# Two-level second product: another order of VectorE's sums, two outer sums left on GpSimd, the first group's weight sums in buffers of their own

## The chip, the cores and the metric

The kernel runs on one core of one Trainium2 chip. The metric is device time in microseconds (us) of one execution. The engines are TensorE (PE; its weight loads are listed as PEld), VectorE (DVE), ScalarE (ACT), GpSimd (POOL) and SyncE (SP), which only issues DMAs here. All data is float32.

## What is computed

Linear attention without softmax, with an RMS norm per head, and behind it a token mixer and a channel mixer. Batch 8, 8 heads of 64, sequence 576:

```python
kv = np.einsum('bhsd,bhse->bhde', k, v)
out = np.einsum('bhsd,bhde->bhse', q, kv)
x = out / np.sqrt(np.mean(out * out, axis=-1, keepdims=True) + 1e-06) * g_norm
# x to (8, 576, 512): heads side by side
h = np.maximum(x.transpose(0, 2, 1) @ w_tok1, 0.0) @ w_tok2     # 576 -> 256 -> 576
u = x + h.transpose(0, 2, 1)
h2 = np.maximum(u @ w_ch1, 0.0) @ w_ch2                         # 512 -> 1536 -> 512
return u + h2
```

The change touches only the channel mixer, the last two matrix products and the sums around them.

## The kernel before

**Stages.** Attention and token mixing fill the first third of the run and leave u in nine groups of 512 rows in DRAM (one per batch element, and one of the remaining 64 rows of all). The channel mixer then takes the groups one after the other. For each it computes v = relu(u @ w_ch1) and then v @ w_ch2, which is added to u.

**Winograd's form of Strassen's product.** Both products are done with seven block products instead of eight. With factors cut in 2 by 2 blocks, four sums of one factor's blocks (S1 to S4) and four of the other's (T1 to T4) are made first, then products numbered 1 to 7, and seven more additions put the result together. Group 0 does this on one level (`channel1_once`, `channel2_once`). Groups 1 to 8 do it on two: each of the seven *outer* products is made of seven *inner* ones, 49 for each matrix product, 98 for a group. One inner product is three matmuls of 128x128x128, which the trace shows as six records.

**Who does which sums.** Sums within one outer product are *inner* sums, sums between the blocks of the whole matrix *outer* sums.

- The weights' sums are made once, during group 0, by `split` (lines 283 to 297). For every outer product it makes three inner sums in a tile, writes the tile to DRAM (`last`, line 293), and leaves a fourth sum to be made in place (`steps[2]`). Later `fetch_sums` (line 679) fetches one tile for each outer product of each group, three ahead, into the three buffers of the pool `sums`. In the kernel before `split` takes its tiles from these same three buffers (`sums_tile`, line 280).
- The sums of the activations u, transposed in the tile uT, are made by `outer_u` and `inner_u` (lines 457 to 463) on VectorE.
- The results of the first product, v, lie in tiles v1 to v7. `outer` (line 614) runs one outer product: the inner products 1, 6, 7 and 4 accumulate in one PSUM bank a, 5 and 3 in b, 2 in c. Behind each product on a the running sum is read out by `read` (line 633): into t1, u2, u3 and then to the result's lower left part. ScalarE copies, or, where a *base* is given (line 704), VectorE reads and adds the base. Three writes by VectorE (`write`, line 642) add b or c to t1, u2 and u3. The next product on a can't start before the read of the last one, and the second on b not before the write of the first. `tmp` has one buffer for t1, two for u2 and one for u3.
- The remaining outer sums of v are made by `padd` (line 712) on GpSimd: v3 += v1, v2 += v1, v1 = v4 + v3 and v7 = v5 + v4, each in two halves of 128x768.
- ScalarE applies the relu to v2, v7 and v1 (`rectify`, line 716). The other outer sums of the second product (`make_a21`, `sum1` to `sum4`) are VectorE's, with the relu of v6 in them.
- The inner sums of v for the second product are made by `inner(o)` (line 760) on VectorE: three in a tile sv (three buffers), and one in place, or in a tile sv3 for outer product 1 (`own`).
- The second product's results r are added to each other (`radd`) and to xg (`xadd`), the tile with u, which is then stored in two halves; `fetch_x` fetches the next group's xg into the same tile.

**Order.** The order of work is written out by hand in *places*. A group has 98 of them, one inner product each. Outer product i of the first matrix product (order 1, 6, 2, 7, 5, 3, 4) has its inner products at places 7i + 0, 1, 3, 4, 6, 9 and 12 for p = 1, 2, 6, 5, 7, 4 and 3 (`PLACE`, line 608); the next outer product fills the gaps. The second matrix product (order 1, 4, 6, 5, 7, 2, 3) follows from place 49 on. `put(place, step)` says behind which inner product a step is issued. In the code b is the group's place 0 in `channel1` and its place 49 in `channel2`, so b + 59 there is place 10 of the next group. Steps at one place are issued in the order of their `put`s. Every engine takes its own instructions strictly in the order in which they are issued, and `keep` holds them in it. The writes of an outer product stand at 7i + 2 (c), 7i + 8 (first use of b) and 7i + 13 (second use of b).

The transposes of the next group (`turn_u`) stand at places 60, 64, 68 and 72, the next group's first sums of uT at 89, 91, 95 and 102, and the fetches of weight sums for the outer product three ahead at 7n + 13.

**The start of the two-level part.** During group 0's second product, `weave` (line 857) issues the steps of group 1's preparation between the products: first the last sums for group 0's own weights, then the in-place sums of the seven weights w_ch1, then the sums of the seven weights w_ch2 with their writes to DRAM. After it come the fetches of xg and of the first three tiles of weight sums (lines 985 to 987), and then the places of group 1.

Of the kernel before, what the change touches and what calls it, by code (L numbers as in the profile page):

```python
# [18 lines left out]
def kernel(  # L19
# [32 lines left out]
    nc = tc.nc  # L52
# [67 lines left out]
    def relu(o, a):  # L120
        keep(nc.scalar.activation(o, a, AF.Relu))  # L121
# [158 lines left out]
    def sums_tile():  # L280
        return late["sums"].tile([P, 3, FQ], F32, name="sums", tag="sums")

    def split(weight, o):


        at = []
        steps = (s_sums if weight == 1 else t_sums)(lambda n: part(weight, o, n, at[0]))

        def first():
            at.append(sums_tile())  # L290
            steps[0]()

        def last():
            steps[3]()
            dma(sums_dram[weight, o], at[0])

        return [first, steps[1], last], steps[2]
# [313 lines left out]
    def put(place, *steps):  # L611
        beside[place] += steps
# [52 lines left out]
    def sub(t, i, j):  # L665

        return t[:, ts(i, W), j]
# [22 lines left out]
    def channel1(g, n0):  # L690


        b = 7 * n0

        def first(i, o):
            n = n0 + i

            def mul(p, ps, start, stop):
                for w in range(W):
                    matmul(ps[:, ts(w, P)], lhsT=part(1, o, p, sums[n])[:, ts(w, P)],  # L700
                           rhs=uT[g][:, SB[o], SB[p]], start=(start and w == 0), stop=stop,
                           skip_group_check=True)

            base = {5: 3, 4: 1}.get(o)
            outer(7 * n, FQ, mul, lambda i, j: sub(v_tile(g, TO[o]), i, j),
                  base and (lambda i, j: sub(v_tile(g, base), i, j)))
            put(7 * n + PLACE[3] + 1, do(fetch_sums, n + 3))

        for i, o in enumerate(ORDER1):
            first(i, o)  # L710

        def padd(o, x, y):
            return halves(lambda i: tensor_add(*(half(v_tile(g, t), i) for t in (o, x, y)),
                                               engine=nc.gpsimd))

        def rectify(t, *places):
            for i in range(2):
                for j in range(2):
                    put(b + places[i], lambda i=i, j=j: relu(*2 * [sub(v_tile(g, t), i, j)]))


        put(b + 22, *padd(3, 3, 1))
        put(b + 29, *padd(2, 2, 1))
        put(b + 36, *padd(1, 4, 3))
        put(b + 43, *padd(7, 5, 4))
        rectify(2, 36, 39)
        rectify(7, 47, 48)
        rectify(1, 57, 58)
        if g > 1:
            steps = outer_u(g) + inner_u(g, 2, 7)  # L730
            for place, step in zip((0, 0, 2, 3, 4, 5, 7, 9), steps):
                put(b + place, step)

    def channel2(g, n0):
        b = 7 * n0
        t = {n: do(v_tile, g, i) for n, i in FROM.items()}

        def second(i, o):
            n = n0 + i
            r = {}  # L740

            def mul(p, ps, start, stop):
                v = v_in_parts[g, o](p)
# [12 lines left out]
            return r  # L756

        rs = {o: second(i, o) for i, o in enumerate(ORDER2)}

        def inner(o):  # L760


            got = {}

            def v_part(p):
                if p in (5, 6, 3):
                    return got[0][:, {5: 0, 6: 1, 3: 2}[p]]
# [12 lines left out]
            def own():  # L780
                a21 = sub(t[o](), 0, 1)
                got[7] = late["s3"].tile([P, W, P], F32, name="sv3")
                tensor_add(got[7], v_part(1), a21, ALU.subtract)

            return [begin, steps[1], steps[3]], own if o == 1 else steps[2]

        ins = {o: inner(o) for o in ORDER2}
        n1, n2, n3, n4, n5, n6, n7 = (t[n] for n in range(1, 8))
        a21 = n7

        def sum1(i):
            keep(nc.vector.scalar_tensor_tensor(out=half(n5(), i), in0=half(a21(), i), scalar=0.0,
                                                in1=half(n4(), i), op0=ALU.max, op1=ALU.add))

        def sum2(i):
            tensor_add(half(n6(), i), half(n5(), i), half(n1(), i), ALU.subtract)

        def sum3(i):

            keep(nc.vector.scalar_tensor_tensor(out=half(n7(), i), in0=half(a21(), i), scalar=0.0,  # L800
                                                in1=half(n1(), i), op0=ALU.max, op1=ALU.subtract))

        def sum4(i):
            tensor_add(half(n3(), i), half(n2(), i), half(n6(), i), ALU.subtract)

        def make_a21(i):
            tensor_add(half(a21(), i), half(a21(), i), half(v_tile(g, 5), i))

        put(b - 8, *ins[1][0], ins[1][1])
        put(b + 1, *halves(make_a21))  # L810
        put(b + 4, *ins[4][0])
        put(b + 6, *halves(sum1))
        put(b + 9, ins[4][1], *halves(sum2))
        put(b + 12, *ins[6][0])
        put(b + 15, *halves(sum4))
        put(b + 17, ins[6][1], *ins[5][0])
        put(b + 20, ins[5][1], *halves(sum3))
        put(b + 24, *ins[7][0], ins[7][1])
        put(b + 28, *ins[2][0], ins[2][1])
        put(b + 33, *ins[3][0], ins[3][1])  # L820


        quarter = lambda i, j: xg[g][:, 2 * i:2 * i + 2, ts(j, DH)]
        radd = lambda o, a: do(lambda: tensor_add(rs[o][0], rs[o][0], rs[a][0]))
        xadd = lambda i, j, o: do(lambda: tensor_add(quarter(i, j), quarter(i, j), rs[o][0]))
        put(b + 22, xadd(0, 0, 1))
        put(b + 23, xadd(1, 0, 4))
        put(b + 29, radd(6, 1))
        put(b + 31, xadd(0, 1, 6))
        put(b + 36, xadd(0, 1, 5))  # L830
        put(b + 38, xadd(1, 1, 5))
        put(b + 43, radd(7, 6))
        put(b + 52, xadd(1, 0, 7), xadd(1, 1, 7))
        put(b + 59, xadd(0, 0, 2), do(store, g, xg, 1))
        put(b + 63, xadd(0, 1, 3), do(store, g, xg, 0), do(fetch_x, g + 1))


        for i in range(J):
            place = b + 12 + 4 * i
            put(place - 12, do(fetch_t, g + 1, i)) if i < 2 else None  # L840
            put(place - 1, do(turn_u, g + 1, i, t_psum))
            put(place, do(fetch_t, g + 1, i + 2)) if i < 2 else None
        for i, step in enumerate(inner_u(g + 1, 0, 2)):

            put(b + (53 if i == 2 else 40 + 2 * i), step)

    def store(g, x, i):
        x = x[g]
# [129 lines left out]
    inner1 = [split(1, o) for o in ORDER1]  # L978
    inner2 = [split(2, o) for o in ORDER2]
    weave(channel1_once(0), firsts + [f for fs, _ in inner1 for f in fs])  # L980
    extra = [do(turn, 1, i, t_psum) for i in range(J)]
    extra += [lambda: [f() for f in outer_u(1)], lambda: [f() for f in inner_u(1, 0, 7)], lambda: None]
    body = [step for pair in zip(channel2_once(0), extra) for step in pair]
    weave(body, lasts + [f for _, f in inner1] + [f for fs, _ in inner2 for f in fs])
    fetch_x(1)
    for n in range(3):
        fetch_sums(n)


    for n, (_, f) in enumerate(inner2):  # L990
# [44 lines left out]
```

## Time and profile before

| | us |
|---|---|
| median of 3 runs | 978.64 |
| the runs | 974.67, 978.64, 981.25 |
| the profiled execution | 981.5 |
| its span, first to last instruction | 979.6 |
| mean granted TensorE clock | 0.945 |

| busy in the span | us | share |
|---|---|---|
| TensorE matmul | 861.8 | 88% |
| VectorE | 724.5 | 74% |
| ScalarE | 331.1 | 34% |
| GpSimd | 122.1 | 12% |

The two-level part goes from 336.6 us to 972 us. The profile's tables name a group of instructions by line, engine, operation and tiles; L118, L121, L124 and L127 are the helpers through which all additions, relus, copies and matmuls go, so the tiles tell them apart: `t<-ps_a,v` is a read of bank a into t1 with a base, `v<-ps_b,u` a write from b, `sv<-sv,v` an inner sum for the second product, `uT<-uT` a sum of the activations. A wait reads: who, for whom, how long in all, how often, the longest one. In the order of time a line gives start, duration, engine, line, operation, shape and count, and in brackets the idle time before it with what ended it.

### The profile page before, as it was taken

To read this page: it belongs to the slowest core of one execution; us is meant where nothing else is said; L and a number is where in the kernel's file an instruction comes from. 1 tells how busy PE (TensorE), PEld (TensorE's weight loads), DVE (VectorE), ACT (ScalarE), POOL (GpSimd) and SP (SyncE) were. 2 spreads that over 40 slices of the span, in tenths; PEclk is the share of its full clock that TensorE was granted. 3 is DMA by queue.
4 is the path that set the end of the run, shared out by engine and by line. 5 is a ranking of instruction groups with operands and counts; after the bars stand their busy time and mean duration, and the time that the engine had idled before them with its cause. 6 is when DMAs were issued, how large, how long until landed. Compare 5 with 4: busy or idle time off the path is not lost.

```text
span 979.6 us, 16051 instructions
## 1 busy us (share of the span) xinstructions
PE 861.8 (88%) x6144; PEld 761.1 (78%) x6144; DVE 724.5 (74%) x1384; ACT 331.1 (34%) x924; POOL 122.1 (12%) x78
## 2 busy tenths in 40 slices
PE   6478997979999868998998999899899799899896
PEld 6255564644588768998998999899899799899896
DVE  2568887988786835985885885886796697598585
ACT  2556545455111022323324223323323233332321
POOL 1000000000000005006006004102302300500600
PEclk9789898989999978999999899899899899999998
DMA  9975776422422453444535444335345344454432
GB/s 306 322 249 183 258 229 221 162 86 96 156 107 90 161 200 99 162 139 157 165 119 186 141 143 162 135 127 184 117 143 187 115 144 143 144 171 140 153 122 68
DMA packets 66924, 156.53 MB, mean 160 GB/s; under 512 B 5280, under 2 KB 23712, under 8 KB 66848
## 3 DMA queue, kind: packets, MB, share of 16 engines
q1 hardware_dynamic: 65488, 154.29, 46.8%
q10 hardware_dynamic: 1360, 1.21, 0.4%
q8 instruction: 49, 0.80, 0.3%
q14 instruction: 27, 0.22, 0.1%
HBM read 128.35 MB, written 27.13 MB: 159 GB/s over the span
## 4 chain that ended last, share of the span: by engine, by line
PE 53%; DVE 28%; DMA 9%; issue 4%; ACT 4%; SPq 0%; DVEq 0%; ACTq 0%
PE ps_a L127 19%; PE ps_b L127 10%; DVE v L118 7%; DVE sv L118 7%; PE ps_u L127 5%; PE ps_h L127 5%; PE ps_c L127 4%; DMA sums<-sums 4%; PE ps_v L127 4%; PE ps_w L127 3%; ACT x L351 2%; DVE xg L118 2%; DVE uT L118 2%; DVE r L118 2%; DMA out_dram<-xg 2%
## 5 line engine op out<-in xcount | busy, mean ns | idle before, releaser
L118 POOL TENSOR_TENSOR v<-v,v 128x768 f32<-128x768 f32 x64 | 119.4, 1892 | 803.9 <-DVE v L118 779.0
L124 ACT COPY u<-ps_a 128x384 f32<-128x384 f32 (+1 forms) x192 | 67.9, 354 | 213.0 <-PE ps_a L127 194.7
L118 DVE TENSOR_TENSOR v<-ps_b,u 128x384 f32<-128x384 f32 x112 | 60.5, 552 | 60.8 <-PE ps_b L127 44.1
L127 PE MATMUL ps_a<-uT,sums 128*128 128x128 f32 x336 | 54.5, 304 | 48.1 <-DVE t L118 30.0
L127 PE MATMUL ps_b<-uT,sums 128*128 128x128 f32 x672 | 95.5, 296 | 0.0
L127 PEld LDWEIGHTS ps_b<-uT,sums 128*128 128x128 f32 x672 | 90.3, 212 | 0.0
L127 PE MATMUL ps_a<-uT,w_ch 128*128 128x128 f32 x576 | 83.5, 286 | 7.0 <-DVE uT L118 7.0
L127 PEld LDWEIGHTS ps_a<-uT,sums 128*128 128x128 f32 x336 | 47.4, 213 | 51.0 <-DVE t L118 31.5
L127 PEld LDWEIGHTS ps_a<-uT,w_ch 128*128 128x128 f32 x576 | 76.0, 202 | 8.2 <-issue 8.1
L351 ACT ACTIVATE x<-x,inv 128x64 f32<-128x64 f32 x288 | 70.9, 335 | 17.0 <-DVE inv L347 16.9
L124 ACT COPY t<-ps_a 128x384 f32<-128x384 f32 (+1 forms) x96 | 34.0, 354 | 124.0 <-PE ps_a L127 123.7
L127 PE MATMUL ps_h<-x,w_tok 128*128 128x512 f32 (+1 forms) x160 | 67.3, 613 | 5.1 <-DVE w_tok L118 5.1
L127 PE MATMUL ps_u<-h,w_tok 128*128 128x512 f32 (+1 forms) x160 | 71.7, 640 | 0.0
L118 DVE TENSOR_TENSOR uT<-uT 128x512 f32<-128x512 f32 (+3 forms) x96 | 62.6, 663 | 2.7 <-ACT uT L124 1.9
L121 ACT ACTIVATE v<-v 128x384 f32<-128x384 f32 (+1 forms) x102 | 49.5, 527 | 28.4 <-DVE v L118 20.0
L127 PE MATMUL ps_a<-uT,w 128*128 128x128 f32 x432 | 59.0, 276 | 0.0
L118 DVE TENSOR_TENSOR u<-ps_a,v 128x384 f32<-128x384 f32 x32 | 17.8, 558 | 52.5 <-PE ps_a L127 52.5
L127 PEld LDWEIGHTS ps_h<-x,w_tok 128*128 128x128 f32 (+1 forms) x160 | 26.8, 195 | 35.8 <-issue 34.2
L127 PEld LDWEIGHTS ps_a<-uT,w 128*128 128x128 f32 x432 | 53.8, 193 | 0.0
L127 PEld LDWEIGHTS ps_u<-h,w_tok 128*128 128x128 f32 (+1 forms) x160 | 27.4, 195 | 33.8 <-issue 31.6
L127 PEld LDWEIGHTS ps_kv<-v_in,k_in 128*128 128x128 f32 x320 | 40.1, 203 | 14.8 <-DMA v_in<-in_v_dram 6.3
L127 PEld LDWEIGHTS ps_o<-kvp,qT 128*128 128x128 f32 x256 | 33.8, 207 | 21.4 <-ACT kvp L124 8.2
(119 smaller groups left out, 1736.9 us busy)
## 6 DMA issues: line engine op xcount, KB each, us to landing
sums<-sums SPq DMA_DIRECT2D x126, 576.0 KB, 3.8
qT<-in_q_dram SPq DMA_DIRECT2D x8, 1152.0 KB, 7.6
xt<-u_dram SPq DMA_DIRECT2D x36, 256.0 KB, 3.3
xg<-u_dram SPq DMA_DIRECT2D x9, 1024.0 KB, 5.7
k_in<-in_k_dram SPq DMA_DIRECT2D x16, 512.0 KB, 5.9
u_dram<-x SPq DMA_DIRECT2D x16, 512.0 KB, 3.1
out_dram<-xg SPq DMA_DIRECT2D x16, 512.0 KB, 3.3
v_in<-in_v_dram SPq DMA_DIRECT2D x14, 512.0 KB, 6.8
```

Of the source, the lines that this page charges most:

```text
L118: keep(engine.tensor_tensor(out=o, in0=a, in1=b, op=op))
L121: keep(nc.scalar.activation(o, a, AF.Relu))
L124: keep(nc.scalar.copy(o, a))
L127: keep(nc.tensor.matmul(*a, **kw))
L351: keep(nc.scalar.activation(x3[:, i], x3[:, i], AF.Copy, scale=inv[:, i]))
```

## The change

- `split` takes its tiles from the pool sv (three buffers, used for the inner sums of v from place 41 of group 1 on, now 32). The fetches of the first three tiles of weight sums are issued before group 0's second product, and in that product's filling the sums of w_ch2 with their writes come ahead of the in-place sums of w_ch1.
- GpSimd keeps v1 = v4 + v3 and v7 = v5 + v4. The sum v3 += v1 becomes VectorE's, at place 24 instead of 22. The sum v2 += v1 is done while outer product 2 is read out: it gets v1 as its base, so its four reads go from ScalarE to VectorE.
- The relus of v2 go from places 36 and 39 to 25, 25, 28 and 29; those of v1 from 57 and 58 to 53, 53, 54 and 57.
- The inner sums for the second product's outer 1 go from place 41 to 32, 32, 33 and 35. Those for the others, and the outer sums between them, are spread over more places, one or two at each, between 50 and 87.
- The first outer sum of the next group's activations goes from the next group's place 0 to 95, and the in-place inner sum is split: for outer 1 it goes to 96, for outer 2 to place 3 of the next group. (Both were at place 4.)
- Additions to xg for outer 7 go from place 101 to 93 and 94, and the store of the second half from 108 to 102. Those for outers 1, 6 and 5 move by one or two places.

```diff
         def first():
-            at.append(sums_tile())
+            at.append(late["sv"].tile([P, 3, FQ], F32, name="sv"))
             steps[0]()
...
-            base = {5: 3, 4: 1}.get(o)
+            base = {2: 1, 5: 3, 4: 1}.get(o)
...
-        put(b + 22, *padd(3, 3, 1))
-        put(b + 29, *padd(2, 2, 1))
-        put(b + 36, *padd(1, 4, 3))
-        put(b + 43, *padd(7, 5, 4))
-        rectify(2, 36, 39)
-        rectify(7, 47, 48)
-        rectify(1, 57, 58)
+        put(b + 24, *add(3, 3, 1))
+        put(b + 36, *add(1, 4, 3, nc.gpsimd))
+        put(b + 43, *add(7, 5, 4, nc.gpsimd))
+        for t, *places in ((2, 25, 29, 28, 25), (7, 47, 47, 48, 48), (1, 53, 57, 53, 54)):
+            for place, (i, j) in zip(places, ((0, 0), (0, 1), (1, 0), (1, 1))):
+                rectify(place, t, i, j)
         if g > 1:
-            steps = outer_u(g) + inner_u(g, 2, 7)
-            for place, step in zip((0, 0, 2, 3, 4, 5, 7, 9), steps):
+            steps = outer_u(g)[1:]
+            for place, step in zip((0, 0, 2, 3, 4, 5, 7, 9), steps + [inner_u(g, 1, 2)[2]] + inner_u(g, 2, 7)):
                 put(b + place, step)
...
-            return [begin, steps[1], steps[3]], own if o == 1 else steps[2]
+            return begin, steps[1], own if o == 1 else steps[2], steps[3]
...
-        put(b - 8, *ins[1][0], ins[1][1])
-        put(b + 1, *halves(make_a21))
-        put(b + 4, *ins[4][0])
-        put(b + 6, *halves(sum1))
-        put(b + 9, ins[4][1], *halves(sum2))
-        put(b + 12, *ins[6][0])
-        put(b + 15, *halves(sum4))
-        put(b + 17, ins[6][1], *ins[5][0])
-        put(b + 20, ins[5][1], *halves(sum3))
-        put(b + 24, *ins[7][0], ins[7][1])
-        put(b + 28, *ins[2][0], ins[2][1])
-        put(b + 33, *ins[3][0], ins[3][1])
...
+        for place, steps in (
+                (-17, [ins[1][0], ins[1][2]]), (-16, [ins[1][1]]), (-14, [ins[1][3]]),
+                (1, [A[0], ins[4][0]]), (2, [A[1]]), (4, [ins[4][1], S1[0]]), (6, [ins[4][3], S1[1]]),
+                (8, [S2[0]]), (9, [ins[4][2], S2[1]]), (11, [ins[6][0]]), (12, [S4[0]]),
+                (13, [ins[6][1], S4[1]]), (15, [ins[6][3], ins[6][2]]), (17, [ins[5][0], S3[0]]),
+                (19, [ins[5][1], S3[1]]), (20, [xadd(0, 0, 1)]), (21, [ins[5][3], ins[5][2]]),
+                (23, [ins[7][0], xadd(1, 0, 4)]), (25, [ins[7][1]]), (26, [ins[7][2], ins[7][3]]),
+                (28, [ins[2][0]]), (29, [radd(6, 1)]), (30, [ins[2][1], xadd(0, 1, 6)]),
+                (32, [ins[2][3], ins[2][2]]), (34, [ins[3][0]]), (36, [xadd(0, 1, 5), ins[3][1]]),
+                (37, [xadd(1, 1, 5)]), (38, [ins[3][3], ins[3][2]]), (43, [radd(7, 6)]),
+                (44, [xadd(1, 0, 7)]), (45, [xadd(1, 1, 7)]), (53, [do(store, g, xg, 1)]),
+                (59, [xadd(0, 0, 2)]), (63, [xadd(0, 1, 3), do(store, g, xg, 0), do(fetch_x, g + 1)])):
+            put(b + place, *steps)
...
-        for i, step in enumerate(inner_u(g + 1, 0, 2)):
-
-            put(b + (53 if i == 2 else 40 + 2 * i), step)
+
+        if g + 1 < NG:
+            first, second, _, fourth = inner_u(g + 1, 0, 2)
+            put(b + 40, first)
+            put(b + 41, second)
+            put(b + 42, fourth)
+            put(b + 46, outer_u(g + 1)[0])
+            put(b + 47, inner_u(g + 1, 0, 1)[2])
...
     weave(channel1_once(0), firsts + [f for fs, _ in inner1 for f in fs])
+    for n in range(3):
+        fetch_sums(n)
...
-    weave(body, lasts + [f for _, f in inner1] + [f for fs, _ in inner2 for f in fs])
+    weave(body, lasts + [f for fs, _ in inner2 for f in fs] + [f for _, f in inner1])
     fetch_x(1)
-    for n in range(3):
-        fetch_sums(n)
```

More of the change, by code (lines that the diff above doesn't have):

```diff
@@ L710, in channel1, with add, rectify @@
             first(i, o)
-        def padd(o, x, y):
+        def add(o, x, y, engine=nc.vector):
             return halves(lambda i: tensor_add(*(half(v_tile(g, t), i) for t in (o, x, y)),
[L714 to L719, printed above, removed]
-        put(b + 22, *padd(3, 3, 1))
-        put(b + 29, *padd(2, 2, 1))
-        put(b + 36, *padd(1, 4, 3))
-        put(b + 43, *padd(7, 5, 4))
-        rectify(2, 36, 39)
-        rectify(7, 47, 48)
-        rectify(1, 57, 58)
+                                               engine=engine))
+        def rectify(place, t, i, j):
+            put(b + place, lambda: relu(*2 * [sub(v_tile(g, t), i, j)]))
+        put(b + 24, *add(3, 3, 1))
[4 more added lines that the diff above has]
+                rectify(place, t, i, j)
         if g > 1:
-            steps = outer_u(g) + inner_u(g, 2, 7)
-            for place, step in zip((0, 0, 2, 3, 4, 5, 7, 9), steps):
+            steps = outer_u(g)[1:]
+            for place, step in zip((0, 0, 2, 3, 4, 5, 7, 9), steps + [inner_u(g, 1, 2)[2]] + inner_u(g, 2, 7)):
                 put(b + place, step)
@@ L825, in channel2 @@
         xadd = lambda i, j, o: do(lambda: tensor_add(quarter(i, j), quarter(i, j), rs[o][0]))
[L826 to L835, printed above, removed]
+        A, S1, S2, S3, S4 = (halves(f) for f in (make_a21, sum1, sum2, sum3, sum4))
+        for place, steps in (
[11 more added lines that the diff above has]
+            put(b + place, *steps)
         for i in range(J):
```

## The prediction

> **What bounds the kernel now.** I read the page first, then the table of TensorE's waits from 336 us on, then a table by stretches of one group each, and last the order of time around each wait.
>
> ```profile
> span 979.6 us, 16051 instructions
> ```
> ```profile
> PE ps_a L127 <- DVE t L118: 30.0, 8, 3.8
> PE ps_a L127 <- DMA sums<-sums: 17.8, 6, 14.0
> PE ps_a L127 <- DVE uT L118: 7.0, 7, 1.0
> PE ps_b L127 <- DVE r L118: 6.9, 8, 1.1
> PE ps_a L127 <- DVE v L118: 2.6, 9, 1.1
> ```
> ```profile
> 428.70:504.90 76.20, 70.32 (x607) 69.30 (x606) 59.31 (x111) 24.45 (x64) 14.93 (x8) 0.98 0.45 151
> 582.20:660.80 78.60, 71.38 (x607) 70.34 (x607) 59.33 (x112) 24.48 (x65) 14.91 (x8) 0.96 0.43 146
> ```
>
> (A row of the last view: stretch, its length, busy time and count of PE, PEld, DVE, ACT and POOL, granted clock, DMA share, GB/s.) The two-level part is bound by TensorE, which issues one product (six matmul records) every 0.67 us (623.10 to 623.77 below) and waits 64 us in all. A group has 98 products, 65.7 us, and takes 76 to 79. The largest row comes once in each of the eight groups, always at the same product: the one 45 places into the group, the second product of outer 4. The fourth group, VectorE, GpSimd and then TensorE:
>
> ```profile
> 612.77 2.04 DVE L118 TENSOR_TENSOR sv<-sv,v 128x384 f32<-128x384 f32 x1
> 614.85 2.04 DVE L118 TENSOR_TENSOR sv<-v,sv 128x384 f32<-128x384 f32 x1
> 617.29 0.55 DVE L118 TENSOR_TENSOR t<-ps_a,v 128x384 f32<-128x384 f32 x1
> ```
> ```profile
> 608.73 7.75 POOL L118 TENSOR_TENSOR v<-v,v 128x768 f32<-128x768 f32 x4 [4.10 <-ACT t L124]
> ```
> ```profile
> 613.31 0.83 PE L127 MATMUL ps_a<-uT,w 128*128 128x128 f32 x6
> 617.89 1.65 PE L127 MATMUL ps_a<-uT,sums 128*128 128x128 f32 x6 [3.75 <-DVE t L118]
> 619.33 2.77 PE L127 MATMUL ps_b<-uT,sums 128*128 128x128 f32 x12
> 621.89 1.37 PE L127 MATMUL ps_a<-uT,w_ch 128*128 128x128 f32 x6
> 623.10 0.83 PE L127 MATMUL ps_a<-w_ch,v 128*128 128x128 f32 x6
> 623.77 0.83 PE L127 MATMUL ps_c<-w_ch,v 128*128 128x128 f32 x6
> ```
> ```profile
> 617.90:624.70 6.80, 6.80 (x39) 6.80 (x40) 2.77 (x6) 0.27 (x1) 0.00 (x0) 0.62 0.24 86
> ```
>
> TensorE needs t, which VectorE reads from PSUM. In VectorE's queue the four sums of the second product's first left operand (sv) stand ahead of it, and the two shown take 2.04 us each while GpSimd works (608.73 to 616.48). The same sum without GpSimd takes 0.56 (row 646.76 below). The wait then costs a second time: in the 6.8 us behind it the granted clock is 0.62 and products come 1.2 to 1.4 us apart. From 613.31 to 623.10 five products take 9.79 us where 3.35 would do: 6.4 us a group.
>
> **Part 1, first left operand of the second product.** The change moves these four sums from place 41 to places 32, 32, 33 and 35, and the relus that they need from 36 and 39 to 25 to 29. GpSimd's first remaining sum (place 36) needs v4, which is written at place 34, so all but the fourth sum are done before GpSimd starts. Nothing is then queued before t at place 42, apart from writes of 0.55 from PSUM. The row 623.10 shows where TensorE would be in step again. In the groups granted 0.98 (second and seventh) the slow stretch is shorter:
>
> ```profile
> 462.98 1.65 PE L127 MATMUL ps_a<-uT,sums 128*128 128x128 f32 x6 [3.75 <-DVE t L118]
> 464.43 2.26 PE L127 MATMUL ps_b<-uT,sums 128*128 128x128 f32 x12
> 466.52 0.83 PE L127 MATMUL ps_a<-uT,w_ch 128*128 128x128 f32 x6
> ```
>
> There three products take 3.54 instead of 2.01, so 1.5 of slow clock and 3.9 of wait (4.58 from 613.31 to 617.89, less 0.67): 5.4. Sum: 6 x 6.4 + 2 x 5.4 = **49 us gained**. The unknown is the fourth sum at place 35, which starts within 0.2 us of GpSimd: either it is first, and GpSimd ends 0.5 later, which t at place 42 still meets, or it is held 1.5 us (2.04 less 0.56), the b write of outer 5 behind it is late for its third product by about 0.8, and 8 groups lose 6. I take nothing, because the write of v4 releases both but VectorE's next instruction follows without a semaphore's way; both ends stay in the range.
>
> The Trainium skill (SBUF — State Buffer, section "SBUF: two separate sides") says that a VectorE instruction with two SBUF inputs and a GpSimd instruction share a port pair that the first to start holds to its end. The trace agrees: 2.04 against 0.56 for two SBUF inputs, 0.55 as ever for t<-ps_a,v. By that rule the fourth sum is a matter of who comes first, and the sum of this part is 49 or 43.
>
> **Part 2, GpSimd's two outer sums on VectorE.** The sum for v2 vanishes as an instruction: its base is added while outer 2 is read from PSUM, so four copies per group leave ScalarE and become VectorE reads.
>
> ```profile
> L118 POOL TENSOR_TENSOR v<-v,v 128x768 f32<-128x768 f32 x64 | 119.4, 1892 | 803.9 <-DVE v L118 779.0 <-ACT t L124 24.9
> ```
> ```profile
> L118 DVE TENSOR_TENSOR v<-ps_b,u 128x384 f32<-128x384 f32 x112 | 60.5, 552 | 60.8 <-PE ps_b L127 44.1 <-ACT u L124 16.6
> ```
> ```profile
> L118 DVE TENSOR_TENSOR v<-v,v 128x768 f32<-128x768 f32 x48 | 43.6, 950 | 0.0
> ```
> ```profile
> L118 DVE TENSOR_TENSOR u<-ps_a,v 128x384 f32<-128x384 f32 x32 | 17.8, 558 | 52.5 <-PE ps_a L127 52.5
> ```
>
> VectorE gets 4 x 0.56 + 2 x 0.95 = 4.1 us a group and loses the 3 in which two sums were held (2 x 1.5): 59.3 becomes 60.4 of some 68. It lies beside TensorE: the idle columns of the PSUM reads (60.8 and 52.5 us, before reads that are all in the first product) say that VectorE waits there for TensorE. A read is needed three places (2.01 us) after its product starts; the product itself is shown with 0.83, the read takes 0.56, so 0.6 is spare. The v3 sum at place 24 has four places, 2.7 us, for 1.9 and one write of 0.55. I take 0. Bounds: nothing, or one read a group held by a whole half of the v3 sum, 0.95 less the spare 0.6, 8 x 0.35, about 3.
>
> **Part 3, the activations' sums.** One outer sum goes to the end of the group before, and the in-place inner sum for outer 1 with it, so the seventh product of outer 1 (place 6) no longer waits:
>
> ```profile
> 586.07 0.91 PE L127 MATMUL ps_a<-uT,w_ch 128*128 128x128 f32 x6 [0.99 <-DVE uT L118]
> ```
>
> By the table of waits that is 7.0 in seven groups: **7 us gained**. The moved work, with two xg additions, comes to some 2 us at the tail of a group; over the second half of a group VectorE is idle for 3.8 us (38.10 less 34.34, next part), most of it at that tail.
>
> **Part 4, VectorE in the second product.** Here it is nearly full, and its late r writes stop TensorE:
>
> ```profile
> 622.70:660.80 38.10, 37.09 (x327) 36.57 (x326) 34.34 (x71) 11.66 (x36) 0.00 (x0) 1.00 0.46 153
> ```
> ```profile
> 635.39 0.48 DVE L118 TENSOR_TENSOR r<-ps_b,u 128x128 f32<-128x128 f32 x2
> 635.79 1.82 DVE L118 TENSOR_TENSOR v<-v,v 128x768 f32<-128x768 f32 x2
> ```
> ```profile
> 646.76 0.56 DVE L118 TENSOR_TENSOR sv<-sv,v 128x384 f32<-128x384 f32 x1
> ```
> ```profile
> 648.30 0.28 DVE L118 TENSOR_TENSOR r<-ps_b,u 128x128 f32<-128x128 f32 x1
> ```
> ```profile
> 648.63 0.94 PE L127 MATMUL ps_b<-d,sv 128*128 128x128 f32 x6 [0.83 <-DVE r L118]
> ```
>
> The same amount of work is spread. Ahead of the write at 648.30 three sums (1.5 us) go behind it, more than the wait. But the two halves of the fourth outer sum (635.79, 1.82) now stand ahead of the write at 635.39, and one sum goes behind: 1.3 later, against about 1.1 spare. I reckon 0.1 there and 0.4 seven places on, 4 us in all instead of 6.9 + 2.6 = 9.5: **5.5 gained**. Bounds: no wait left (9.5), or 1.5 a group (loss 2.5).
>
> **Part 5, the start.**
>
> ```profile
> 334.60 4.21 DVE L118 TENSOR_TENSOR uT<-uT 128x896 f32<-128x896 f32 x4
> ```
> ```profile
> 343.93 0.55 DVE L118 TENSOR_TENSOR v<-ps_c,t 128x384 f32<-128x384 f32 x1
> ```
> ```profile
> 344.09 3.60 SPq L115 DMA_DIRECT2D sums<-sums  x3
> ```
> ```profile
> 337.31 0.83 PE L127 MATMUL ps_c<-uT,w_ch 128*128 128x128 f32 x6
> 352.12 1.62 PE L127 MATMUL ps_a<-uT,sums 128*128 128x128 f32 x6 [13.98 <-DMA sums<-sums]
> ```
> ```profile
> 357.09 0.83 PE L127 MATMUL ps_c<-uT,w 128*128 128x128 f32 x6
> ```
>
> The first weight sums are fetched behind all writes of sums and behind xg. With buffers of their own they are fetched before group 0's second product, 30 us ahead, on SP behind seven writes that are done by then. The cost now: 13.98, and 352.12 to 357.09 is four products in 4.97 instead of 2.68: 16.3. What is late next is VectorE: after uT (338.8) come seven in-place weight sums and two more (9 x 0.47 start to start) and one xg addition (0.6) before v<-ps_c,t, which ends near 344.1; ScalarE's copy to the same t (0.48) follows at 344.6, and TensorE would want it at 337.98 + 6 x 0.67 = 342.0. That leaves 2.7: **13.6 gained** (11 if the clock falls again, 16 without a wait).
>
> The known waits end in a granted clock of 0.62 at 3.75 us, and do not at 1.5. The Trainium skill (TensorE: Matmul & The Clock Gate, section "What's actually happening") puts the limit at one idle window of about 3.4 us. By it 2.7 costs nothing more; by the rows alone it may cost another 2.3.
>
> **Part 6, the wait for weights at place 31** stays:
>
> ```profile
> 604.53 0.91 PE L127 MATMUL ps_a<-uT,sums 128*128 128x128 f32 x6 [1.47 <-DMA sums<-sums]
> ```
>
> It follows the store of xg's first half and the fetch of the next xg on SP; both keep their places. The addition before that store comes some 1 us later, behind a read. I take 0 (bounds: 3.8 gained, 7 lost).
>
> **Sum**: 49 + 7 + 5.5 + 13.6 = 75 off 979.6, 904.6 of span. Around it lie 1.9 us (981.5 profiled); the median of the runs, 978.64, is 2.9 under that. So 981.5 - 75 - 2.9 = 903.6, **904 us**.
>
> **Rivals.** *VectorE full*: in the second product it was busy 34.34 of 38.10, and a shorter group leaves no slack; waits of 2 a group where I have 0.5: +12, 916. *GpSimd sets t*: v1 comes from its sum of two halves, 3.8 us from place 36; by the row 608.73 its two halves end near 612.5 (2 x 1.89), before t, but within about 1 us of when t would be read without the sums ahead. Held and late so that the whole wait stays: 904 + 49 = 953. *Weights late*: with 1.47 now, 2 more in seven groups falls in with the slow clock (2.5): 7 x 4.5 = 31, 935. *Start not cured* (the first fetch waits on anyway): 904 + 14, 918. *The other side*: GpSimd's last sum slides into the opening of the second product, which TensorE now reaches sooner. Each of its four halves can hold a two-input VectorE sum 1.5 us, 6 a group, and a TensorE wait of 3.75 brings 2.5 of slow clock; with two such waits a group (2 x 6.4) it costs 102, 1006. It decides when GpSimd's last half ends past place 50, and the rows speak against it: started at place 36, four halves of 1.89 take 7.6 us, 11 places, and end near place 47. *Nothing changes*, the wait moving whole from t to another read: 979.
>
> **Chances.** Forecast 0.60; VectorE full 0.13; t by GpSimd 0.07; weights late 0.07; start 0.05; slower 0.05; no change 0.03. The forecast's own range is 888 to 912: below, 904 less all waits left in parts 4 to 6 (4, 2.7 and 3.8), less 3.3 for the spread of the runs (974.67 to 981.25) and 2 for the slow clock, which I read to 0.3 us a group; above, the losses of parts 1 and 5 (6 and 2.3). To take in full VectorE, the start and late weights the range is 888 to 938. One per cent is about what a measurement here tells from none: faster than that 0.91, within it 0.04, slower 0.05.
>
> **What would show it.** Right: no TensorE wait for t; sv sums all near 0.56; granted clock 1.00 through every group; groups of 68 to 70 us; the start waits 2 to 3 us for VectorE or ScalarE, not DMA; GpSimd at half its 119 us. Wrong: a wait over 3 us that comes back each group, VectorE without gaps from place 14 to 98, or a sv sum of 2 us at place 50.

## The result, and the profile after

The changed kernel takes **899.32 us** (median of 4 runs, 898.42 to 899.91) against 978.74 us of the kernel before (4 runs, 974.67 to 981.25): a ratio of 0.919, 95% interval 0.916 to 0.922. Forecast were 904, with 888 to 912 as the forecast's own range. The profiled execution took 898.4, its span 896.6; the span of before was 979.6, so 83.0 us are to be explained.

The page after, its first line and the granted clock in 40 slices:

```profile
span 896.6 us, 15996 instructions
...
PEclk9789899998999999999999999999999999999999
```

From the sixteenth slice on, where the two-level part begins, every digit is 9 (90% or more). TensorE's waits from 330 us on (who, for whom, sum, count, longest):

```profile
PE ps_a L127 <- DMA sums<-sums: 5.5, 7, 1.6
PE ps_a L127 <- DVE v L118: 2.9, 8, 0.7
PE ps_a L127 <- ACT t L124: 2.2, 1, 2.2
PE ps_b L127 <- DVE r L118: 0.5, 1, 0.5
PE ps_a L127 <- ACT u L124: 0.4, 1, 0.4
```

64 us of waits have become 11.5. The rows for t by VectorE (30.0) and for uT (7.0) are gone, r has fallen from 6.9 to 0.5, and sums from 17.8 to 5.5, with no wait of 14 us among them. What is left on top is the wait for weights at place 31, which the change didn't touch. Two groups, the second and the fourth, and then the fourth one's second product, from its second place on:

```profile
406.60:475.20 68.60, 67.85 (x606) 67.53 (x605) 58.57 (x118) 22.63 (x60) 7.29 (x4) 1.00 0.51 168
544.20:613.90 69.70, 67.81 (x606) 67.48 (x605) 58.48 (x118) 22.61 (x60) 7.28 (x4) 1.00 0.49 165
578.50:613.90 35.40, 35.08 (x315) 34.92 (x314) 34.53 (x74) 11.60 (x36) 0.00 (x0) 1.00 0.51 170
```

A group takes 68.6 to 69.8 us from the second on (76 to 79 before) at a clock of 1.00, and GpSimd works half as long in it. In the second product VectorE is busy 34.53 of 35.40 us: almost nothing is left there, and TensorE waits for it in each group (the row `v`; 0.55 us from start to start).

The place that cost most, in the fourth group: VectorE, GpSimd and TensorE around the first left operand of the second product.

```profile
567.68 0.55 DVE L118 TENSOR_TENSOR sv<-sv,v 128x384 f32<-128x384 f32 x1
568.28 0.56 DVE L118 TENSOR_TENSOR u<-ps_a,v 128x384 f32<-128x384 f32 x1
568.75 0.55 DVE L118 TENSOR_TENSOR v<-ps_b,u 128x384 f32<-128x384 f32 x1
569.22 0.55 DVE L118 TENSOR_TENSOR sv<-v,sv 128x384 f32<-128x384 f32 x1
...
573.70 0.56 DVE L118 TENSOR_TENSOR t<-ps_a,v 128x384 f32<-128x384 f32 x1 [0.84 <-PE ps_a L127]
```
```profile
569.47 7.28 POOL L118 TENSOR_TENSOR v<-v,v 128x768 f32<-128x768 f32 x4 [62.49 <-ACT t L124]
```
```profile
573.44 0.83 PE L127 MATMUL ps_c<-uT,w_ch 128*128 128x128 f32 x6
574.11 0.83 PE L127 MATMUL ps_a<-uT,w 128*128 128x128 f32 x6
```

The last of the four sums starts at 569.22, a quarter of a microsecond ahead of GpSimd, and takes 0.55. Before t is read VectorE now waits for TensorE (0.84), where TensorE had waited for it, and the products go on 0.67 apart. What the forecast left open, who comes first at place 35, is answered: VectorE.

The start of group 1, VectorE, ScalarE and TensorE:

```profile
342.70 0.55 DVE L118 TENSOR_TENSOR v<-ps_c,t 128x384 f32<-128x384 f32 x1
```
```profile
343.34 0.48 ACT L124 COPY t<-ps_a 128x384 f32<-128x384 f32 x1 [3.20 <-DVE v L118]
```
```profile
340.80 0.83 PE L127 MATMUL ps_a<-uT,w_ch 128*128 128x128 f32 x6
343.87 0.94 PE L127 MATMUL ps_a<-uT,sums 128*128 128x128 f32 x6 [2.24 <-ACT t L124]
```

The 14 us for the weights are gone, and what was named as late next is late: VectorE's v<-ps_c,t, behind it ScalarE's copy to t, and TensorE with 2.24 us (2.40 from start to start, 2.7 forecast).

### The profile page after: what moved, and what is told of

It is laid out like the page before. It is cut to its first block, busy times and chain, and to the rows that moved or that the text cites. A ratio compares the mean times of both kernels' runs of the same rounds, so it can differ in the third digit from the quotient of the medians.

```text
span 896.6 us, 15996 instructions
## 1 busy us (share of the span) xinstructions
PE 834.0 (93%) x6144; PEld 738.4 (82%) x6144; DVE 717.7 (80%) x1439; ACT 316.7 (35%) x892; POOL 61.1 (7%) x46
## 4 chain that ended last, share of the span: by engine, by line
PE 67%; DVE 16%; DMA 11%; ACT 4%; issue 1%; DVEq 0%; ACTq 0%; SPq 0%
PE ps_a L127 26%; PE ps_b L127 13%; PE ps_c L127 6%; DMA sums<-sums 6%; PE ps_u L127 5%; PE ps_h L127 5%; DVE v L118 4%; PE ps_v L127 4%; PE ps_w L127 3%; DMA k_in<-in_k_dram 2%; ACT x L351 2%; DVE sv L118 2%; DMA v_in<-in_v_dram 2%; DVE v L789 2%; PE ps_ut L453 1%
## 5 line engine op out<-in xcount | busy, mean ns | idle before, releaser
L124 ACT COPY u<-ps_a 128x128 f32<-128x128 f32 (+1 forms) x176 | 60.3, 343 | 177.9 <-PE ps_a L127 166.0
L118 POOL TENSOR_TENSOR v<-v,v 128x768 f32<-128x768 f32 x32 | 58.3, 1849 | 790.5 <-ACT t L124 790.4
L127 PE MATMUL ps_b<-uT,sums 128*128 128x128 f32 x672 | 85.5, 275 | 0.0
L127 PEld LDWEIGHTS ps_b<-uT,sums 128*128 128x128 f32 x672 | 80.2, 192 | 0.0
L127 PE MATMUL ps_a<-uT,w_ch 128*128 128x128 f32 x576 | 78.8, 275 | 0.0
L124 ACT COPY t<-ps_a 128x128 f32<-128x128 f32 (+1 forms) x88 | 30.2, 343 | 100.7 <-PE ps_a L127 92.6
L118 DVE TENSOR_TENSOR uT<-uT 128x512 f32<-128x512 f32 (+4 forms) x103 | 63.1, 629 | 2.9 <-ACT uT L124 1.9
L118 DVE TENSOR_TENSOR v<-v,v 128x768 f32<-128x768 f32 (+1 forms) x70 | 64.3, 927 | 0.3
L118 DVE TENSOR_TENSOR u<-ps_a,v 128x384 f32<-128x384 f32 x48 | 26.8, 558 | 39.7 <-PE ps_a L127 39.3
L127 PE MATMUL ps_a<-uT,sums 128*128 128x128 f32 x336 | 47.4, 277 | 7.7 <-DMA sums<-sums 5.5
```

Source lines behind the costliest of these rows:

```text
L118: keep(engine.tensor_tensor(out=o, in0=a, in1=b, op=op))
L124: keep(nc.scalar.copy(o, a))
L127: keep(nc.tensor.matmul(*a, **kw))
```

## The experiments

The theory is that of the forecast: the gain is the sum of four separate waits. Its main rival is that one of them does it all, by GpSimd: with two sums fewer it holds VectorE less, and where the sums stand is of no account. The kernel before, measured again beside each set of runs, had medians of 975.9 to 980.9; the ratios are to it. Where two runs of different sets are compared, a difference of 2 us is within that scatter.

**1. Only the order of the first left operand undone** (place 41 again):

```diff
-                (-17, [ins[1][0], ins[1][2]]), (-16, [ins[1][1]]), (-14, [ins[1][3]]),
+                (-8, [ins[1][0], ins[1][1], ins[1][3], ins[1][2]]),
```

> The changed kernel with only the four sums of the second product's first left operand put back to place 41. Theory (they are held by GpSimd's halves there, and t is queued behind them): two of them take about 2.0 us again, TensorE waits 3.5 to 4 us for t in each group, the clock falls behind it, 6 us a group: 944 to 952 us. Rival (the gain came from halving GpSimd's work and spreading VectorE's, not from this move): under 905 us.

Measured: 946.02 us, 0.969 (0.966 to 0.972): 46.7 more than the changed kernel. TensorE's waits, VectorE and TensorE of this kernel:

```profile
PE ps_a L127 <- DVE t L118: 29.5, 8, 3.7
```
```profile
594.79 2.04 DVE L118 TENSOR_TENSOR sv<-v,sv 128x384 f32<-128x384 f32 x1
596.76 0.55 DVE L118 TENSOR_TENSOR sv<-v 128x384 f32<-128x384 f32 x1
597.23 0.54 DVE L118 TENSOR_TENSOR t<-ps_a,v 128x384 f32<-128x384 f32 x1
```
```profile
597.83 1.65 PE L127 MATMUL ps_a<-uT,sums 128*128 128x128 f32 x6 [3.69 <-DVE t L118]
```

The wait is back as it was (29.5 in all and 3.7 at most; before 30.0 and 3.8), the product behind it slow again (1.65), although GpSimd has only two of its four sums left. The rival that fewer sums do it falls.

**2. The same, and GpSimd without any outer sum.** To the edit of 1:

```diff
-        put(b + 36, *add(1, 4, 3, nc.gpsimd))
-        put(b + 43, *add(7, 5, 4, nc.gpsimd))
+        put(b + 36, *add(1, 4, 3))
+        put(b + 43, *add(7, 5, 4))
```

> As the run before, and GpSimd's two remaining sums on VectorE at their own places, so that GpSimd does nothing in the groups. Theory (held): no sum above 0.6 us, t late by at most 1.5 us and no fall of the clock, in spite of four sums and two halves more in VectorE's queue: 903 to 915 us. Rival (the place in the queue alone makes t late, held or not): a wait of over 3 us and the slow clock stay, 940 us or more.

Measured: 914.71 us, 0.937 (0.936 to 0.939). The waits and the same sum:

```profile
PE ps_a L127 <- DVE u L118: 6.8, 8, 0.9
...
PE ps_a L127 <- DVE t L118: 4.8, 8, 0.6
```
```profile
579.92 0.56 DVE L118 TENSOR_TENSOR sv<-v,sv 128x384 f32<-128x384 f32 x1
```

The same order, the same place, and the sum takes 0.56 instead of 2.04; the wait for t falls from 3.7 to 0.6, and no group behind the first has a step at half clock. GpSimd's holding makes the wait, the order decides whether it reaches TensorE.

**3. The new order, and GpSimd without any outer sum** (the edit of 2 alone).

> The changed kernel with GpSimd's two remaining sums on VectorE at places 36 and 43. VectorE gets 3.5 us more a group where it idles 3.9 us (places 36 to 48), between the reads of outer product 4. Theory: each half may make one read late by 0.3 to 0.8: 900 to 908 us. Rival (what GpSimd still does disturbs VectorE more than it helps): under 898 us.

Measured: 905.61 us, 0.928 (0.926 to 0.929). One row is new among the waits:

```profile
PE ps_a L127 <- DVE u L118: 3.4, 8, 0.4
```

With runs 1 to 3 and the changed kernel both factors are crossed. The old order costs 46.7 us with GpSimd's two sums (946.0 against 899.3) and 9.1 without (914.7 against 905.6). Taking the last two sums from GpSimd costs 6.3 in the new order and gains 31.3 in the old one.

**4. The kernel before, with these sums later instead of sooner**, behind t as well (place 48):

```diff
-        put(b - 8, *ins[1][0], ins[1][1])
+        put(b - 1, *ins[1][0], ins[1][1])
```

> The kernel before with one edit: the first left operand's sums go from place 41 to 48, where GpSimd is nearly done; GpSimd keeps all its four outer sums. Theory: the wait for t and its slow clock go (49 us), but 2.1 us of VectorE's work move into the opening of the second product, where its late writes cost 1 to 3 us more a group: 940 to 960 us. Rival (GpSimd's load as such): 975 to 981 us.

Measured: 948.64 us, 0.972 (0.970 to 0.973), 27 us faster by one changed number. Among its waits from 330 us on:

```profile
PE ps_b L127 <- DVE r L118: 13.8, 16, 1.2
```

No wait for t is left, but r has doubled, from 6.9 to 13.8: the sums now load VectorE in the second product, where it has no room. The half group there takes 38.5 us from start to start instead of 36.4, 17 us of the 51 given back (the profiled executions lie 32.7 apart, and the wait at place 31 took another 1.9). So "ahead of t" was the better way out, and the load in the second product is a limit of its own.

**5. The start undone**: tiles from the pool sums, the first fetches behind group 0, w_ch1 ahead of w_ch2.

```diff
-            at.append(late["sv"].tile([P, 3, FQ], F32, name="sv"))
+            at.append(sums_tile())
...
-    for n in range(3):
-        fetch_sums(n)
...
-    weave(body, lasts + [f for fs, _ in inner2 for f in fs] + [f for _, f in inner1])
+    weave(body, lasts + [f for _, f in inner1] + [f for fs, _ in inner2 for f in fs])
     fetch_x(1)
+    for n in range(3):
+        fetch_sums(n)
```

> The changed kernel with the start as it was: weight sums made in the fetch buffers, the first fetches behind group 0's second product, in-place sums of w_ch1 ahead of the sums of w_ch2. Theory: TensorE waits 14 us for the first weight sums again instead of 2.4, with some 2.3 us of slow clock: 911 to 915 us. Rival (the wait is VectorE's and only changes its name): 899 to 904 us.

Measured: 912.09 us, 0.930 (0.927 to 0.933): 12.8 more, where 13.6 were forecast. The wait is the old one, 14.3 us, once; the other seven in its row are those at place 31:

```profile
PE ps_a L127 <- DMA sums<-sums: 18.7, 8, 14.3
```

**6. The second product's sums bunched again as before**, with the first left operand where the change put it; most additions to r and xg go back to their places too. The core of the edit:

```diff
-                (1, [A[0], ins[4][0]]), (2, [A[1]]), (4, [ins[4][1], S1[0]]), (6, [ins[4][3], S1[1]]),
+                (1, A), (4, [ins[4][0], ins[4][1], ins[4][3]]), (6, S1), (9, [ins[4][2]] + S2),
...
```

> The changed kernel with VectorE's sums of the second product (places 50 to 87) in bunches as before; the first left operand's sums stay at 32 to 35. Theory: late r writes stop TensorE by 1.0 to 1.4 us a group instead of 0.5: 903 to 911 us. Rival (the stretch is TensorE's, and the order of equal work doesn't matter): 898 to 901 us.

Measured: 909.45 us, 0.928 (0.926 to 0.931): 10.1 more. The old row returns as it was:

```profile
PE ps_b L127 <- DVE r L118: 6.9, 8, 1.1
```

So the spread, the moved additions included, is worth 10 us, not the 5.5 of the forecast.

**7. One sum given back to GpSimd** (v3 += v1, at 22 as before):

```diff
-        put(b + 24, *add(3, 3, 1))
+        put(b + 22, *add(3, 3, 1, nc.gpsimd))
```

> The changed kernel with the outer sum v3 += v1 on GpSimd again, at place 22, where VectorE does only sums that read PSUM. Theory: nothing of VectorE's is held there and VectorE has slack there: no difference, 897 to 902 us. Rival (VectorE's load sets the pace, so 1.9 us less a group tell): under 893 us. Other rival (any GpSimd sum costs by being late): over 906 us.

Measured: 898.07 us, 0.916 (0.914 to 0.919), which can't be told from the changed kernel. That GpSimd has two sums only is worth nothing by itself for this one; for v2, whose sum is part of the reads now, it wasn't tried.

**8. The activations' sums back** (place 0 and, the in-place one, place 4):

```diff
-            steps = outer_u(g)[1:]
-            for place, step in zip((0, 0, 2, 3, 4, 5, 7, 9), steps + [inner_u(g, 1, 2)[2]] + inner_u(g, 2, 7)):
+            steps = outer_u(g)
+            for place, step in zip((0, 0, 2, 3, 4, 5, 7, 9), steps + inner_u(g, 2, 7)):
...
-            put(b + 46, outer_u(g + 1)[0])
-            put(b + 47, inner_u(g + 1, 0, 1)[2])
+            put(b + 53, third)
```

> The changed kernel with the sums of the next group's activations where they were: the first outer sum at place 0, the in-place inner sum for outers 1 and 2 at place 4. Theory: TensorE waits about 1 us at place 6 in seven groups: 905 to 909 us. Rival (with the xg additions gone from the group's start VectorE comes round in time all the same): 898 to 902 us.

Measured: 898.53 us, 0.917 (0.914 to 0.920): nothing lost, and no wait for uT, where 905 to 909 was expected. Here the forecast's reason for its 7 us falls. VectorE at the opening of the fourth group shows what else had changed, two additions to xg that are not there any more:

```profile
544.47 3.34 DVE L118 TENSOR_TENSOR uT<-uT 128x512 f32<-128x512 f32 x5
```

**9 and 10. The additions to xg back** (outer 7, place 101), alone and together with the edit of 8. The new theory: the additions stood ahead of the in-place sum, 1.2 us of VectorE, and either move alone takes away the wait.

```diff
-                (44, [xadd(1, 0, 7)]), (45, [xadd(1, 1, 7)]), (53,
+                (52, [xadd(1, 0, 7), xadd(1, 1, 7)]), (53,
```

> After the run with the activations' sums put back had shown no wait at place 6: the changed kernel with only the two additions of outer 7 to xg put back from places 93 and 94 to 101. New theory (either move alone is enough, since the in-place sum is wanted 1.0 us late and each move takes about 1.2 us off what stands ahead of it, or takes the sum away from there): no wait at place 6, 897 to 902 us. Rival (the xg additions alone were the cause): about 1 us of wait in seven groups, 905 to 909 us.

> Both put back: the activations' sums to places 0 and 4, and the two additions to xg to place 101. New theory (the wait needs both): about 1 us of wait for uT in seven groups, 905 to 909 us. Rival (neither made it; the lag came from VectorE's stretch in the second product, which is now spread): 897 to 902 us.

Measured: 900.89 us alone (0.920, 0.917 to 0.923), with no wait for uT; 908.38 together (0.929, 0.926 to 0.931). In the second, TensorE's wait and VectorE at the same opening:

```profile
PE ps_a L127 <- DVE uT L118: 7.0, 7, 1.0
```
```profile
547.52 0.68 DVE L118 TENSOR_TENSOR uT<-uT 128x512 f32<-128x512 f32 x1
548.12 1.29 DVE L118 TENSOR_TENSOR xg<-xg,r 128x512 f32<-128x512 f32 x2
549.32 2.74 DVE L118 TENSOR_TENSOR uT<-uT 128x512 f32<-128x512 f32 x4
```

The seven waits are there again only with both edits. The new theory stands: 9.1 us for the pair, of which 1.0 is a longer tail (see the table below), 0 for the one move, and for the other nothing that can be told from the runs' spread. The rival, that VectorE's load in the second product made the wait, falls: in run 10 that load is spread, and the wait is there.

**11. The next group's xg fetched 14 places later** (place 28 instead of 14), since the wait at place 31 is what remains. This goes beyond both kernels:

```diff
-                (59, [xadd(0, 0, 2)]), (63, [xadd(0, 1, 3), do(store, g, xg, 0), do(fetch_x, g + 1)])):
+                (59, [xadd(0, 0, 2)]), (63, [xadd(0, 1, 3), do(store, g, xg, 0)])):
             put(b + place, *steps)
+        put(b + 77, do(fetch_x, g + 1))
```

> A new version: the changed kernel with one step moved, the fetch of the next group's xg from place 14 to 28, so that the weight sums for outer 5 (wanted at place 31) no longer stand behind it in SP's queue, where it waits for the store of the same buffer. Theory: the 5.5 us of waits for weights at place 31 go, about 7 us with what follows them: 891 to 895 us. Rival (they wait for the DMA engines' bandwidth, not for the queue): 897 to 901 us.

Measured: **891.25 us** (5 runs, 890.51 to 892.86), 0.912 (0.909 to 0.914). SP's own waits from 330 us on, in the changed kernel and then in this one:

```profile
SPq L115 <- DMA out_dram<-xg: 20.6, 8, 3.4
```
```profile
SPq L115 <- DMA out_dram<-xg: 2.9, 1, 2.9
```

The fetch of xg goes into the tile that the store reads, so it waits for the store to land, up to 3.4 us, and the fetch of the weights stood behind it on SP. In TensorE's table the row for sums is gone and the others are as they were.

What this run doesn't separate is the queue from the transfer. In the fourth group of the changed kernel the weights for place 31 are fetched right behind xg, and they also take longer to land than in this run, where they are fetched ahead of xg. SP in the changed kernel, the landing of the second row's fetch, and that of the same weights in run 11:

```profile
558.14 0.37 SPq L115 DMA_DIRECT2D xg<-u_dram  x1
558.60 0.46 SPq L115 DMA_DIRECT2D sums<-sums  x1
```
```profile
DMA to landing us min/median/max: 6.6/6.6/6.6
```
```profile
DMA to landing us min/median/max: 3.7/3.7/3.7
```

Over the seven groups with this wait, the fetch was issued some 1.1 us later than in run 11, counted from the group's start (2.2 in the fourth), and took 2.5 to 3.8 us longer. The waits were 0.5 to 1.7 from start to start: the slower landing alone is longer than each of them, the later issue than all but one. So the rival (the DMA engines' bandwidth) is not excluded; no run moved the one without the other.

**12. On top of 11, the start and place 62**: the in-place sums of w_ch1 spread over group 1, and one in-place sum for outer 4 a place sooner.

```diff
-    weave(body, lasts + [f for fs, _ in inner2 for f in fs] + [f for _, f in inner1])
+    weave(body, lasts + [f for fs, _ in inner2 for f in fs] + [inner1[0][1]])
...
-                (8, [S2[0]]), (9, [ins[4][2], S2[1]]), (11, [ins[6][0]]), (12, [S4[0]]),
+                (8, [ins[4][2], S2[0]]), (9, [S2[1]]), (11, [ins[6][0]]), (12, [S4[0]]),
...
```

> As the run before, and two more: the in-place sum for the second product's outer 4 ahead of the fifth outer sum's first half (place 57) instead of behind it, and most of the in-place weight sums of group 1 spread over its places 4 to 46 instead of standing in one bunch ahead of its first write. Theory: the 0.5 us wait of every group at place 62 goes (4 us) and so does the 2.4 us wait at the start: 884 to 890 us. Rival (VectorE is full there and other late writes take their place): 890 to 895 us.

Measured: 890.81 us, 0.911 (0.909 to 0.914): not to be told from run 11, and not the 884 to 890 of the theory. The waits at place 62 are gone from the table, but place 66 comes 0.3 us late in their stead, so a group is only 0.17 shorter, as the rival had it. The start's wait is still there under another name, now for the very sums that were spread (at 339.76, with half clock behind it):

```profile
PE ps_a L127 <- DVE w_ch L118: 2.5, 1, 2.5
```

## Why the prediction was right

The time fell where it was forecast, five of the six parts within 2 us. By the order of time of TensorE's products (each start to the next, less 0.67) the profiled execution gained:

| part | forecast | profiled execution | undone by itself, medians |
|---|---|---|---|
| 1 first left operand | 49 | 50.6 | 46.7 (run 1) |
| 2 outer sums on VectorE | 0 | 0 | 0 (run 7, one of the two) |
| 3 activations' sums | 7 | 8.6 | 9.1 (run 10, with xg and its tail of 1.0) |
| 4 spread in the second product | 5.5 | 9.6 | 10.1 (run 6) |
| 5 start | 13.6 | 13.6 | 12.8 (run 5) |
| 6 weights at place 31 | 0 | -1.3 | not tried |
| sum | 75 | 81.1 | |

The other 1.9 of the 83.0 lie outside: the two-level part began 0.85 sooner and its tail was 1.0 shorter. The first can't be put down to the change, for over the changed kernel and its variants that start scatters by 3.5 us (333.3 to 336.8). The tail can, and the forecast has no term for it: from the start of the last product to the end of the span it is 7.5 us now and 8.5 before, and 8.5 again in runs 9 and 10, which put the additions of outer 7 to xg back to place 101. The forecast took the median 2.9 under the profiled execution, as it was before; after, it lies 0.9 above, and that gives back 3.8 of the 8.0 by which the parts and this rest beat the 75. To that extent it is luck that the median came out only 4.7 from the forecast.

*Part 1* held in mechanism and size, and its open end came out on the gain's side: the fourth sum starts ahead of GpSimd, and all 56 of each kind are short, where each kind took 43 us before:

```profile
L118 DVE TENSOR_TENSOR sv<-sv,v 128x384 f32<-128x384 f32 x56 | 30.8, 550 | 0.0
...
L118 DVE TENSOR_TENSOR sv<-v,sv 128x384 f32<-128x384 f32 x56 | 30.8, 550 | 0.0
```

The lock that the Trainium skill names (SBUF — State Buffer, section "SBUF: two separate sides") is borne out by runs 1 and 2, which differ only in the engine that does the last two outer sums: 2.04 against 0.56 for two SBUF inputs. The forecast's third figure there, 0.55 for t<-ps_a,v, does not show that a read of PSUM goes free, since in the kernel before that read (617.29) comes after GpSimd's end (616.48); the same read at 573.70 above does, with 0.56 while GpSimd works. The late product, which the forecast calls the second of outer 4, is its second on bank a and its third in order. Run 4 shows that a place behind t cures the wait too, and why it is the worse one.

*Part 2* was right at zero. No TensorE wait for a u by VectorE stands in the table. VectorE's time in a group came to 58.5, not 60.4: instructions behind one another overlap (569.22 above takes 0.55, and the next write starts 0.46 later), so added durations count too much.

*Part 3* had the right wait and half of the cause. The step that failed is the sentence that the wait goes because the in-place sum is moved, with the two xg additions named only as load at the tail. Runs 8 to 10 show that each of the two moves is enough; VectorE was 1.2 us late at place 6, and either move takes away enough. The size was low for the reason of part 4.

*Part 4* is the term that was mis-sized. What is left was forecast at 4 us and is 5.9 (0.55 in each of seven groups, 2.0 in the last), though not where it was looked for: the writes behind the fourth outer sum are in time, and the wait is at place 62, for a sum of v. What was there to be gained was taken from the table of waits, 9.5, and that counts only idle time; from start to start it was 15.4. Three rows of before show it, a late product with its neighbours:

```profile
646.97 0.83 PE L127 MATMUL ps_b<-sums,sv 128*128 128x128 f32 x6
648.63 0.94 PE L127 MATMUL ps_b<-d,sv 128*128 128x128 f32 x6 [0.83 <-DVE r L118]
649.41 0.83 PE L127 MATMUL ps_a<-w_ch,v 128*128 128x128 f32 x6
```

The wait has 0.83, but from 646.97 to 649.41 two products take 2.44 instead of 1.34, 1.10 late. Parts 1 and 5 were read from start to start and came out; parts 3 and 4 were read from the idle column and came out low by 5.7 together, nearly all that the sum missed.

*Part 5* held: 2.40 of wait for 2.7, at the place and for the engines named. Whether the clock falls behind it, which the forecast left at 0 to 2.3, is told below.

*Part 6* lost 1.3, inside its bounds. In the fourth group, TensorE:

```profile
565.33 0.91 PE L127 MATMUL ps_a<-uT,sums 128*128 128x128 f32 x6 [1.58 <-DMA sums<-sums]
```

Run 11 bears on the cause that the forecast named, the store and the fetch of xg ahead on SP: with the fetch elsewhere the row is gone, and 8.1 us with it. How much of that is the place in the queue and how much the transfers that run beside each other stays open.

Of the rivals, a full VectorE was the nearest: 34.53 of 35.40 busy, but the wait is 0.55 a group, not 2. GpSimd stayed clear of t (VectorE's read of t ended on TensorE) and of the second product (569.47 + 7.28 = 576.75, and the second product starts at 577.46).

## What to carry to other kernels

Read a wait from the start of one instruction to the start of the next, not from the idle column alone: here the column had two thirds of what two waits cost (16.5 of 24.0 us). A VectorE sum that stands in front of a PSUM read on TensorE's path should be done before GpSimd's work begins or be kept off its hours, and where two pieces of work stand ahead of a late one, try each by itself before naming the cause. Ask also of each late transfer what stood ahead of it in its queue and what moved beside it: issuing one fetch behind the weights' fetch instead of ahead of it was worth 8 us and one line.

## What was not expected of the hardware

The granted clock fell behind shorter waits than the forecast allowed for, and not every time. The start's wait is 2.2 us in ten of the profiled executions; in five it is followed by 3.4 us at half clock, in the others, the changed kernel's among them, by none. The clock changes in steps of 3.4 us on a grid of its own, and what lies in one such step tells the two apart. Two pairs of steps of run 3, at the start and in the fourth group:

```profile
339.40:342.80 3.40, 1.46 (x13) 1.46 (x14) 3.40 (x8) 1.34 (x3) 0.00 (x0) 1.00 0.35 45
342.80:346.20 3.40, 3.40 (x19) 3.40 (x18) 1.75 (x4) 0.48 (x1) 0.00 (x0) 0.50 0.92 309
564.70:568.10 3.40, 1.14 (x10) 1.10 (x10) 0.38 (x2) 0.48 (x1) 0.00 (x0) 1.00 0.77 313
568.10:571.50 3.40, 3.40 (x18) 3.40 (x17) 1.84 (x4) 0.00 (x0) 0.00 (x0) 0.50 0.15 20
```

A step in the changed kernel's start, and the same one of run 1:

```profile
342.30:345.70 3.40, 1.83 (x16) 1.83 (x17) 3.40 (x9) 1.34 (x3) 0.00 (x0) 1.00 0.37 100
345.70:349.10 3.40, 3.40 (x32) 3.40 (x32) 2.77 (x6) 0.71 (x2) 0.00 (x0) 1.00 1.02 370
```
```profile
340.70:344.10 3.40, 1.48 (x13) 1.48 (x14) 3.40 (x8) 1.34 (x3) 0.00 (x0) 1.00 0.40 108
344.10:347.50 3.40, 3.40 (x33) 3.40 (x32) 2.86 (x7) 0.48 (x1) 0.00 (x0) 1.00 0.96 327
```

In these, with TensorE busy 1.14 or 1.46 of 3.40 us the next step is at 0.50, with 1.48 or 1.83 it is at 1.00; at 1.00 it is also behind 1.56 in run 11's start and behind 1.75 in run 4, around a wait of 1.80. So a wait of about 2 us costs up to 1.7 more or nothing, by where it falls in the grid. The Trainium skill (TensorE: Matmul & The Clock Gate, section "What's actually happening") has the clock fall after an idle window; the window's length and that it runs freely agree with the rows, but a window with 43% of TensorE's time in it (1.46 of 3.40) was enough here, so "by it 2.7 costs nothing more" in the forecast does not hold for every execution. 1.46 and 1.48 lie closer together than the place of a step is read here (0.1 us), so if it is the busy time that decides, the limit for these products is near 1.5 of 3.4 us. Whether it is that, no run was made for; in the first stage, with larger matmuls, a step of run 12 with 1.42 kept the clock.
